# Expert batches of 416 places in place of 448 in a fused mLSTM, mixture-of-experts and MLP kernel

## The chip, the core and the metric

The kernel runs on one core of one Trainium2 chip. The metric is the device time of one execution in microseconds (us); three executions of the kernel before took 549.67, 539.68 and 545.39 us, so the median is 545.39 us.

## The reference

Three layers follow each other, all in float32. An mLSTM layer (2 batches, 8 heads, 768 steps, head size 40) gives 1536 tokens of 320 numbers. A mixture of 8 experts then routes each token to two of them, and a dense MLP of width 2048 with a gated ReLU6 closes:

```python
noisy_logits = x @ w_gate + log1p(exp(x @ w_noise)) * noise      # 1536 x 8
top2 = argpartition(-noisy_logits, 2, axis=1)[:, :2]
top2_w = softmax over the two chosen logits
for e in range(8):
    for k in range(2):
        mask = top2[:, k] == e
        h = maximum(x[mask] @ w1[e], 0)                          # 320 -> 1024
        out[mask] += top2_w[mask, k, None] * (h @ w2[e])         # 1024 -> 320
h = out @ w_in                                                   # 320 -> 2048
y = (h * clip(h + 3, 0, 6) / 6) @ w_out                          # 2048 -> 320
```

How many tokens an expert gets depends on the data; 3072 choices fall on 8 experts, 384 each on the mean.

## The kernel before, in words

**Attention and routing.** The loop over 12 chunks of 128 tokens (64 steps of both batches) computes the mLSTM. Each chunk's tokens are written to a DRAM table `Xd`, and `route` (line 428) computes the two experts of each token and a place in each of them. `scatter` (line 412) writes the token's number into the DRAM table `tab` at that place. `CAP` (line 31) is the number of places of one expert. A token whose place is `CAP` or more goes into an overflow part of the table. `overflow` (line 944) holds code under a run-time condition, which handles such tokens in tiles of 128, one after the other; it runs only if some expert has tokens beyond its places.

**Experts.** A `unit` (line 732) is a batch of one expert: a list of tiles (first place, number of places), and `nf` steps of 128 hidden columns. There are 10 such units up to `M0` (line 754): expert 0's first 192 places, expert 1's first 256, expert 1's rest (192 places), experts 2 to 7 with all 448 places (tiles of 128, 128, 128 and 64), and expert 0's rest (256 places in two tiles). `gather` (line 764) fetches a tile's tokens with an indirect DMA issued by GpSimd into `XG`; `xsplit` (line 777) turns each tile with three TensorE transposes (line 783) and splits the result in a high half `XH` and a low half `XL`.

`L1` (line 836) is the first layer of one step: eight matmuls (line 846) with 128x128 stationary weights, in which all of the unit's places move (N columns: 448, 256 or 192). ScalarE writes the high half of the ReLU to `hb` (line 849), VectorE the low half (lines 852, 855 and 857). `L2` (line 868) is the second layer: for each tile of 128 places three matmuls with 320 moving columns, in which the stationary operand is the tile's high half (line 882), again the high half (line 883) and its low half (line 884). A last tile of 64 places takes two: line 886, whose 128 stationary columns are 64 high and 64 low halves side by side, and line 887 with the 64 high halves. For this `L1` lays the last tile's low half right behind the high halves (`u.half`, line 740).

The steps run in a fixed program order (lines 1214 to 1225): `L1` of a step, then `L2` of the step two before it (`LAG`), and between them background work that the tables of lines 1146 to 1213 attach to a step: weights of the next expert (`w_split`: DMA into a ring of four `raw` buffers, ScalarE copy, VectorE subtraction, lines 594 and 595), the conversion of the MLP's weights (`conv`), gathers and transposes of the next unit. At a unit's last step `finish` (line 893) copies the sums out of PSUM and writes them to the DRAM table `Yd` (line 919).

**The MLP.** Six units of 512 tokens follow. `ygather` (line 790) fetches each token's two expert rows from `Yd`, `combine` (line 801) adds them with their weights, and the steps are as above with 512 or, in the first unit, 256 moving columns.

Of the kernel before, what the change touches and what calls it, by code (L numbers as in the profile page):

```python
# [18 lines left out]
OP = mybir.AluOpType  # L19
# [6 lines left out]
DM = H * D  # L26
# [1 line left out]
F = 1024  # L28
FF = 2048
V1 = D + 1  # L30
CAP = 448
CUT = (6, 8)
PRE = (192, 256)
RAWB = 4
# [14 lines left out]
WS = ((-1, 0), (0, 3), (0, 4), (0, 5, 'h'), (1, 0, 'l'), (1, 1), (1, 1), (1, 3), (1, 5), (1, 7), (2, 1))  # L49
TROWS = CAP + 11 * 128  # L50
OVB = 22
# [17 lines left out]
def mlstm_moe_mlp(ctx, tc, qk, kv, on, gf, gf6, wg, nz, w1, w2, w_in, w_out, cf, cb, cs, ci, out):  # L69
    nc = tc.nc  # L70
    V, A, G, T = nc.vector, nc.scalar, nc.gpsimd, nc.tensor
# [8 lines left out]
    def bank(i, dt=F32):  # L80
        return ps.tile([128, 512], dt, name=f"bank{i}")
# [142 lines left out]
    def step(k=1):  # L224
        for _ in range(k):
            for g_ in list(gens):
                if next(g_, "end") == "end":
                    gens.remove(g_)
# [139 lines left out]
    Xd = dram.tile([SLOTS, XW], F32, name="Xd")  # L368
    Yd = dram.tile([OV + CAP * E, DM], F32, name="Yd")
    tab = dram.tile([TROWS * E, 1], I32, name="tab")  # L370
# [54 lines left out]
    def small(shape, name, dt=F32):  # L425
        return const.tile(shape, dt, name=name, bufs=2)

    def route(m):
# [57 lines left out]
        if m == 2:  # L486
            t = small([128, 1], "t7")
            V.tensor_scalar(t, pc[:, 0:1], float(8 * LATE), float(8 * (CAP - LATE)), OP.is_gt, OP.mult)
            yield
# [13 lines left out]
        if 2 * m < 4:  # L503
            hi = small([128, 2, 1], "hi")
            V.tensor_scalar(hi, pe[:, :, 0:1], float(8 * LATE), float(8 * (CAP - LATE)), OP.is_ge, OP.mult)
            yield
# [26 lines left out]
        if m == NT // 2 - 1:  # L533
# [7 lines left out]
            yield  # L541
            V.tensor_scalar(cni[:, 0], cni[:, 0], float(CAP), 0.0, OP.subtract, OP.max)
            yield
# [15 lines left out]
            yield  # L559
            V.scalar_tensor_tensor(SLY, SLE, float(CAP), SLY, OP.mult, OP.add)  # L560
            yield
# [170 lines left out]
    def unit(e, tiles, nf=8):  # L732
        u = U()
        u.e, u.tiles, u.nf = e, tiles, nf
        u.N = sum(n for _, n in tiles)
        u.off, o = [], 0
        for _, n in tiles:
            u.off.append(o)
            o += n
        u.half = u.N - 64 if tiles[-1][1] == 64 else None  # L740
        u.bg = {}
        u.xo = 0
        u.st = e % 2
        u.l1 = [0, 1, 7]
        return u

    full = [(0, 128), (128, 128), (256, 128), (384, 64)]
    first, first2 = [(0, 128), (128, 64)], [(0, 128), (128, 128)]
    rest, rest2 = [(192, 128), (320, 128)], [(256, 128), (384, 64)]
    units = [unit(0, first), unit(1, first2), unit(1, rest2)]  # L750
    units[1].xo = 2
    units += [unit(e, full) for e in range(2, E)] + [unit(0, rest)]
    units[3].xo = 2
    M0 = len(units)
    units += [unit(8 + t, [((4 * t + i) * 128, 128) for i in range(4)]) for g in range(2) for t in range(3)]
    for i, u in enumerate(units):
        u.i = i
        u.g, u.xb = (i - M0) // 3, i % 2 if i < M0 else (i - M0) % 3
        n = len(u.tiles)
# [56 lines left out]
    def weights(u, f):  # L816
        g = f % 8
        if u.e < 8:
            W1 = W2 = sets[u.st]
            o = 5120  # L820
        else:
            W1, W2, o = win(u.g), wout(u.g), 0
        c = [W1[:, x + g * 128:x + g * 128 + 128] for x in (0, 1024, 2048, 3072, 4096)]
        return c, W2[:, o + g * DM:o + g * DM + DM], W2[:, o + 2560 + g * DM:o + 2560 + g * DM + DM]
# [5 lines left out]
    def split_hb():  # L830
        while unsplit:
            hb, r, N = unsplit.pop(0)
            A.copy(hb[:, 0:N], r)  # L833
            V.tensor_tensor(hb[:, N:2 * N], r, hb[:, 0:N], OP.subtract)  # L834

    def L1(u, f, t0, t1):
        (h0, h1, l0, l1, st), _, _ = weights(u, f)
        c0, N = u.off[t0], sum(n for _, n in u.tiles[t0:t1])
        p = bank(u.l1[nl1[0] % len(u.l1)])[:, 0:N]
        nl1[0] += 1  # L840
        xh, xl = [t[:, :, c0:c0 + N] for t in (XH[u.xb], XL[u.xb])]
        ops = [(h0, xh[:, 0]), (h0, xl[:, 0]), (l0, xh[:, 0]),
               (h1, xh[:, 1]), (h1, xl[:, 1]), (l1, xh[:, 1]),
               (st, xh[:, 2]), (st, xl[:, 2])]
        for i, (a, b) in enumerate(ops):
            T.matmul(p, a, b, start=(i == 0), stop=(i == 7))  # L846
        hb = wp.tile([128, 1024], F32R, name="hb", bufs=3)
        if u.e < 8:
            A.activation(hb[:, 0:N], p, AF.Relu)  # L849
            step()  # L850
            if u.half is None:
                V.scalar_tensor_tensor(hb[:, N:2 * N], p, 0.0, hb[:, 0:N], OP.max, OP.subtract)
            else:
                o = u.half
                V.scalar_tensor_tensor(hb[:, N:N + 64], p[:, o:N], 0.0, hb[:, o:N], OP.max, OP.subtract)  # L855
                step()
                V.scalar_tensor_tensor(hb[:, N + 64:2 * N], p[:, 0:o], 0.0, hb[:, 0:o], OP.max, OP.subtract)
        else:
            r = late.tile([128, 512], F32, name="r6", bufs=2)[:, 0:N]
            A.activation(r, p, AF.Relu, bias=three)  # L860
            V.scalar_tensor_tensor(r, r, 6.0, p, OP.min, OP.mult)  # L861

            split_hb()
            unsplit.append((hb, r, N))
        step()
        return hb

    def L2(u, f, t0, t1, hb, tiles=None):
        if any(h is hb for h, _, _ in unsplit):
            split_hb()  # L870
        _, wh, wl = weights(u, f)
        N = sum(n for _, n in u.tiles[t0:t1])
        if f == 0 and t0 == 0:
            u.acc = [bank(b) for b in (2, 3, 4, 6)[:len(u.tiles)]]
        s, t = f == 0, f == u.nf - 1
        for i in tiles or range(t0, t1):
            n, o = u.tiles[i][1], u.off[i] - u.off[t0]
            if n == 128:
                h = hb[:, o:o + 128]
                lo = N + o + (64 if u.half is not None else 0)  # L880
                p = u.acc[i][:, 0:DM]
                T.matmul(p, h, wh, start=s, stop=False)  # L882
                T.matmul(p, h, wl, start=False, stop=False)  # L883
                T.matmul(p, hb[:, lo:lo + 128], wh, start=False, stop=t)  # L884
            else:
                T.matmul(u.acc[i][:, 0:DM], hb[:, o:o + 128], wh, start=s, stop=False, skip_group_check=True)  # L886
                T.matmul(u.acc[i][0:64, 0:DM], hb[:, o:o + 64], wl, start=False, stop=t, skip_group_check=True)  # L887

    outr = out.rearrange("(b k t) d -> k b t d", b=B, k=NT)

# [2 lines left out]
    def finish(u, tiles=None):  # L893
        for i, (s, n) in enumerate(u.tiles):
            if tiles and i not in tiles:
                continue
            if u.e >= 8:
                if not parts:
                    parts.append(wp.tile([128, 5120], F32, name="SA1"))
                part = parts[0][:, s // 128 * DM:(s // 128 + 1) * DM]  # L900
            if u.e >= 8 and u.g == 0:

                if i % 2:
                    V.tensor_scalar(part, u.acc[i][:, 0:DM], 1.0 / 6.0, None, OP.mult)
                else:
                    A.mul(part, u.acc[i][:, 0:DM], 1.0 / 6.0)
                continue
            y = wp.tile([128, DM], F32, name="yo", bufs=4)
            if u.e < 8:
                if n == 64:  # L910
                    y2 = wp.tile([64, DM], F32, name="yo2", bufs=1)
                    A.copy(y2, u.acc[i][64:128, 0:DM])
                    V.tensor_tensor(y[0:64], u.acc[i][0:64, 0:DM], y2, OP.add)
                elif i % 2:
                    V.tensor_copy(y, u.acc[i][:, 0:DM])
                else:
                    A.copy(y, u.acc[i][:, 0:DM])
                r = OV + (7 - u.e) * CAP + s
                nc.sync.dma_start(Yd[r:r + n], y[0:n])
            else:  # L920
                V.scalar_tensor_tensor(y, u.acc[i][:, 0:DM], 1.0 / 6.0, part, OP.mult, OP.add)  # L921
                k = s // 128

                for b in range(B):
                    (A if b and u is units[-1] else nc.sync).dma_start(outr[k, b], y[rows[b]])
# [145 lines left out]
    n = NT - 2  # L1071
# [142 lines left out]
    for u in units:  # L1214
        if u.i == M0 - 2:
            overflow()
        for t, (f, lo, hi) in enumerate(u.steps):
# [6 lines left out]
            for fn, a in u.bg.get(t, []):  # L1224
                fn(*a)
    v, w = hbs
    L2(*v, (0, 1, 2))
    L2(*w, (0, 1))
    finish(units[-1], (0, 1))
    L2(*v, (3,))  # L1230
    L2(*w, (2, 3))
# [66 lines left out]
```

## Time and profile before

| | |
|---|---|
| three runs | 549.67, 539.68, 545.39 us; median 545.39 us |
| span of the profiled execution, first to last instruction | 546.7 us |
| TensorE (PE) matmuls | 512.1 us, 94% of the span, 4159 instructions |
| VectorE (DVE) | 346.8 us, 63% |
| ScalarE (ACT) | 227.2 us, 42% |
| GpSimd (POOL) | 133.6 us, 24% |
| attention and routing | 0 to 122.2 us |
| ten expert units | 122.2 to 362.1 us |
| six MLP units | 362.1 to 546.7 us |

No more is known of the profiled execution's time than its span. The page rests on one execution; PE's busy time overlaps from one matmul to the next, so that what a matmul costs is read from the distance of two starts, not from its duration. PEld is the load of the stationary operand, which runs beside the matmuls.

### The profile page before, as it was taken

The page shows a single profiled execution, that of the slowest core. Times are in us where ns is not written, and L with a number is a line of the kernel's source. Part 1 is how long each engine was busy: PE and PEld are TensorE (multiplying, and loading weights), DVE is VectorE, ACT ScalarE, POOL GpSimd, SP SyncE. Part 2 cuts the span into 40 slices and gives each one's busy share as a digit, 9 for nine tenths or more (in the row PEclk, how much of TensorE's full clock was granted, in tenths as well). Part 3 has the DMA queues.
Part 4 walks back from the last instruction along what each step waited for, and adds up shares of the span by engine and source line. Part 5 has one row for each costly group of instructions (what it writes and reads, how often), then busy time and mean ns, then how long its engine had stood idle before and what let it go on. Part 6 is the DMA issues. An engine that isn't in the chain of part 4 may idle for free. (4 is left out here: it accounts for less than half of the span.)

```text
span 546.7 us, 10810 instructions
## 1 busy us (share of the span) xinstructions
PE 512.1 (94%) x4159; PEld 455.3 (83%) x4159; DVE 346.8 (63%) x841; ACT 227.2 (42%) x469; POOL 133.6 (24%) x164
## 2 busy tenths in 40 slices
PE   4898989896959999999999999999999999999996
PEld 1476767675959999999999999989989989999985
DVE  5178786667645587878787878457698434343433
ACT  5123534233524354545454544246563333333321
POOL 5163464463530320202020002258600100000000
PEclk9798555568879999999999999999999999999999
DMA  8668788524186379787878768785931700011011
GB/s 237 165 185 232 182 154 148 114 93 117 41 269 214 111 272 285 281 289 274 285 276 290 253 174 295 237 271 172 320 110 74 217 0 1 1 25 24 13 37 49
DMA packets 47207, 92.75 MB, mean 170 GB/s; under 512 B 7488, under 2 KB 30880, under 8 KB 47152
## 3 DMA queue, kind: packets, MB, share of 16 engines
q1 hardware_dynamic: 39020, 68.97, 41.9%
q0 software_dynamic: 6464, 19.94, 12.0%
q10 hardware_dynamic: 1668, 3.12, 1.9%
q8 instruction: 33, 0.54, 0.4%
q14 instruction: 22, 0.18, 0.1%
HBM read 68.73 MB, written 23.07 MB: 168 GB/s over the span
## 5 line engine op out<-in xcount | busy, mean ns | idle before, releaser
L861 DVE SCALAR_TENSOR_TENSOR r<-r,bank 128x512 f32<-128x512 f32 (+1 forms) x56 | 34.2, 610 | 79.8 <-ACT r L860 79.4
L846 PE MATMUL bank<-XH,SB 128*128 128x448 f32 (+3 forms) x280 | 78.2, 350 | 0.3 <-PEq L946 0.3
L849 ACT ACTIVATE hb<-bank 128x448 fp32r<-128x448 f32 (+2 forms) x80 | 37.3, 468 | 93.1 <-PE bank L846 77.8
L860 ACT ACTIVATE r<-bank,cft 128x512 f32<-128x512 f32 (+1 forms) x56 | 35.1, 627 | 95.6 <-PE bank L846 90.0
L846 PE MATMUL bank<-XL,SB 128*128 128x448 f32 (+3 forms) x192 | 68.4, 356 | 0.0
L773 POOL DMA_INDIRECT XG<-Xd,idx x32 | 32.8, 1026 | 138.2 <-PE bank L783 108.4
L882 PE MATMUL bank<-SB,hb 128*128 128x320 f32 x192 | 62.4, 325 | 1.0 <-ACT hb L833 1.0
L882 PE MATMUL bank<-SA,hb 128*128 128x320 f32 x192 | 61.0, 317 | 0.0
L884 PE MATMUL bank<-SB,hb 128*128 128x320 f32 x192 | 60.0, 313 | 0.0
L883 PE MATMUL bank<-SB,hb 128*128 128x320 f32 x192 | 59.7, 311 | 0.0
L884 PE MATMUL bank<-SA,hb 128*128 128x320 f32 x192 | 59.6, 310 | 0.1
L883 PE MATMUL bank<-SA,hb 128*128 128x320 f32 x192 | 59.4, 309 | 0.0
L846 PEld LDWEIGHTS bank<-XH,SB 128*128 128x128 f32 x280 | 51.0, 191 | 5.1 <-issue 0.6
L846 PE MATMUL bank<-XH,SA 128*128 128x448 f32 (+2 forms) x200 | 52.4, 335 | 0.0
L846 PE MATMUL bank<-XL,SA 128*128 128x448 f32 (+2 forms) x120 | 40.1, 335 | 0.1
L846 PEld LDWEIGHTS bank<-XL,SB 128*128 128x128 f32 x192 | 36.6, 190 | 2.8
L882 PEld LDWEIGHTS bank<-SB,hb 128*128 128x128 f32 x192 | 36.6, 191 | 2.4 <-ACT hb L833 1.2
L846 PEld LDWEIGHTS bank<-XH,SA 128*128 128x128 f32 x200 | 36.0, 193 | 2.1 <-ACT XH L784 0.4
L855 DVE SCALAR_TENSOR_TENSOR hb<-bank,hb 128x64 fp32r<-128x64 f32 x64 | 14.1, 220 | 36.8 <-ACT hb L849 36.8
L882 PEld LDWEIGHTS bank<-SA,hb 128*128 128x128 f32 x192 | 36.3, 189 | 1.3
L883 PEld LDWEIGHTS bank<-SB,hb 128*128 128x128 f32 x192 | 36.6, 191 | 0.8
L883 PEld LDWEIGHTS bank<-SA,hb 128*128 128x128 f32 x192 | 36.3, 189 | 1.1
(198 smaller groups left out, 1148.4 us busy)
## 6 DMA issues: line engine op xcount, KB each, us to landing
raw<-in_w_dram SPq DMA_DIRECT2D x18, 640.0 KB
raw<-in_w_dram SPq DMA_DIRECT2D x18, 512.0 KB
qk<-in_qk_dram SPq DMA_DIRECT2D x22, 240.0 KB
craw<-in_w_in_dram SPq DMA_DIRECT2D x8, 640.0 KB
craw<-in_w_out_dram SPq DMA_DIRECT2D x8, 640.0 KB
raw<-in_w_dram SPq DMA_DIRECT2D x18, 256.0 KB
Yd<-yo SPq DMA_DIRECT2D x24, 160.0 KB
kv<-in_kv_dram SPq DMA_DIRECT2D x11, 324.0 KB
```

What stands on the lines that cost most here:

```text
L773: G.indirect_dma_start(out=XG[0:n, (u.xo + i) % 4, :], out_offset=None, in_=Xd[0:CUT[u.i] * 128] if early else Xd[:, :], in_offset=bass.In ...
L846: T.matmul(p, a, b, start=(i == 0), stop=(i == 7))
L849: A.activation(hb[:, 0:N], p, AF.Relu)
L855: V.scalar_tensor_tensor(hb[:, N:N + 64], p[:, o:N], 0.0, hb[:, o:N], OP.max, OP.subtract)
L860: A.activation(r, p, AF.Relu, bias=three)
L861: V.scalar_tensor_tensor(r, r, 6.0, p, OP.min, OP.mult)
L882: T.matmul(p, h, wh, start=s, stop=False)
L883: T.matmul(p, h, wl, start=False, stop=False)
L884: T.matmul(p, hb[:, lo:lo + 128], wh, start=False, stop=t)
```

## The change

Each expert has 416 places. The full units have tiles of 128, 128, 128 and 32 places; expert 1's rest has 128 and 32 (160 places), expert 0's rest 128 and 96 (224 places); the first parts of experts 0 and 1 stay at 192 and 256. A last tile of 32 places is handled as the last tile of 64 was: its high and low halves stand in 64 stationary columns (line 887 of the changed kernel), its high halves alone in 32 (line 888). A tile of 96 is handled as one of 128. The program's instructions stand in the same order and number on every engine; what differs is their sizes. Lines behind 740 are one further down.

```diff
-CAP = 448
+CAP = 416
...
-        u.half = u.N - 64 if tiles[-1][1] == 64 else None
+        u.tail = tiles[-1][1] if tiles[-1][1] < 96 else 0
+        u.half = u.N - u.tail if u.tail else None
...
-    full = [(0, 128), (128, 128), (256, 128), (384, 64)]
+    full = [(0, 128), (128, 128), (256, 128), (384, 32)]
     first, first2 = [(0, 128), (128, 64)], [(0, 128), (128, 128)]
-    rest, rest2 = [(192, 128), (320, 128)], [(256, 128), (384, 64)]
+    rest, rest2 = [(192, 128), (320, 96)], [(256, 128), (384, 32)]
...
-                V.scalar_tensor_tensor(hb[:, N:N + 64], p[:, o:N], 0.0, hb[:, o:N], OP.max, OP.subtract)
+                V.scalar_tensor_tensor(hb[:, N:N + u.tail], p[:, o:N], 0.0, hb[:, o:N], OP.max, OP.subtract)
                 step()
-                V.scalar_tensor_tensor(hb[:, N + 64:2 * N], p[:, 0:o], 0.0, hb[:, 0:o], OP.max, OP.subtract)
+                V.scalar_tensor_tensor(hb[:, N + u.tail:2 * N], p[:, 0:o], 0.0, hb[:, 0:o], OP.max, OP.subtract)
...
-            if n == 128:
-                h = hb[:, o:o + 128]
-                lo = N + o + (64 if u.half is not None else 0)
-                p = u.acc[i][:, 0:DM]
+            if n >= 96:
+                h = hb[:, o:o + n]
+                lo = N + o + u.tail
+                p = u.acc[i][0:n, 0:DM]
                 T.matmul(p, h, wh, start=s, stop=False)
                 T.matmul(p, h, wl, start=False, stop=False)
-                T.matmul(p, hb[:, lo:lo + 128], wh, start=False, stop=t)
+                T.matmul(p, hb[:, lo:lo + n], wh, start=False, stop=t)
             else:
-                T.matmul(u.acc[i][:, 0:DM], hb[:, o:o + 128], wh, start=s, stop=False, skip_group_check=True)
-                T.matmul(u.acc[i][0:64, 0:DM], hb[:, o:o + 64], wl, start=False, stop=t, skip_group_check=True)
+                T.matmul(u.acc[i][0:2 * n, 0:DM], hb[:, o:o + 2 * n], wh, start=s, stop=False, skip_group_check=True)
+                T.matmul(u.acc[i][0:n, 0:DM], hb[:, o:o + n], wl, start=False, stop=t, skip_group_check=True)
...
-                if n == 64:
+                if n < 96:
                     y2 = wp.tile([64, DM], F32, name="yo2", bufs=1)
-                    A.copy(y2, u.acc[i][64:128, 0:DM])
-                    V.tensor_tensor(y[0:64], u.acc[i][0:64, 0:DM], y2, OP.add)
+                    A.copy(y2[0:n], u.acc[i][n:2 * n, 0:DM])
+                    V.tensor_tensor(y[0:n], u.acc[i][0:n, 0:DM], y2[0:n], OP.add)
                 elif i % 2:
-                    V.tensor_copy(y, u.acc[i][:, 0:DM])
+                    V.tensor_copy(y[0:n], u.acc[i][0:n, 0:DM])
                 else:
-                    A.copy(y, u.acc[i][:, 0:DM])
+                    A.copy(y[0:n], u.acc[i][0:n, 0:DM])
```

## Rows read from the trace of the kernel before

**Rows 1.** Page, part 1: busy us, share of the span, instructions.

```profile
span 546.7 us, 10810 instructions
PE 512.1 (94%) x4159; PEld 455.3 (83%) x4159; DVE 346.8 (63%) x841; ACT 227.2 (42%) x469; POOL 133.6 (24%) x164
```

**Rows 2.** Busy time by stage: from:to, us, engines' busy us, PEclk, DMA share, GB/s.

```profile
0.00:122.20 122.20, 104.99 (x1655) 75.13 (x1655) 79.26 (x243) 43.33 (x133) 56.21 (x71) 0.69 0.69 169
122.20:142.80 20.60, 15.29 (x111) 14.33 (x111) 13.54 (x79) 8.17 (x19) 10.86 (x17) 0.83 0.37 104
142.80:166.40 23.60, 17.96 (x118) 17.23 (x117) 12.06 (x28) 8.87 (x17) 7.72 (x10) 0.86 0.57 176
166.40:181.10 14.70, 14.70 (x120) 14.47 (x119) 8.61 (x27) 6.59 (x15) 2.73 (x3) 1.00 0.65 211
...
234.20:261.60 27.40, 27.40 (x166) 25.84 (x166) 21.71 (x44) 13.55 (x22) 3.91 (x4) 1.00 0.82 281
...
345.10:362.10 17.00, 17.00 (x132) 16.98 (x130) 7.70 (x19) 6.30 (x16) 8.23 (x9) 1.00 0.69 227
```

**Rows 3.** Waits from 181 to 362 us: who for whom, us, times, longest.

```profile
ACT hb L849 <- PE bank L846: 62.0, 40, 3.2
POOL raw L697 <- DMA Wi<-clr: 33.6, 1, 33.6
...
POOL yg L794 <- PE bank L846: 12.3, 1, 12.3
...
PE bank L846 <- PEq L946: 0.3, 1, 0.3
```

**Rows 4.** Chain that ended last, pieces of line 846: start us, us.

```profile
338.46 1.61 PE bank L846 x8
...
342.02 1.65 PE bank L846 x8
...
352.48 0.96 PE bank L846 x8
...
466.01 1.84 PE bank L846 x8
```

**Rows 5.** PE in order of time, expert 1's rest: start us, us, instruction.

```profile
179.52 0.25 PE L846 MATMUL bank<-XH,SB 128*128 128x192 f32 x1
179.61 0.27 PE L846 MATMUL bank<-XL,SB 128*128 128x192 f32 x1
...
180.39 0.33 PE L882 MATMUL bank<-SB,hb 128*128 128x320 f32 x1
```

**Rows 6.** PE in order of time, expert 7: end of a second layer.

```profile
337.72 0.31 PE L883 MATMUL bank<-SB,hb 128*128 128x320 f32 x1
337.87 0.31 PE L884 MATMUL bank<-SB,hb 128*128 128x320 f32 x1
338.01 0.30 PE L886 MATMUL bank<-SB,hb 128*128 128x320 f32 x1
338.15 0.31 PE L887 MATMUL bank<-SB,hb 128*64 128x320 f32 x1
338.30 0.36 PE L846 MATMUL bank<-XH,SB 128*128 128x448 f32 x1
```

**Rows 7.** PE in order of time, expert 5: transposes of 128 and of 64 rows.

```profile
279.91 0.37 PE L846 MATMUL bank<-XL,SB 128*128 128x448 f32 x1
280.12 0.49 PE L783 MATMUL bank<-cft,XG 128*128 128x128 f32 x3
280.36 0.39 PE L882 MATMUL bank<-SB,hb 128*128 128x320 f32 x1
...
283.46 0.37 PE L846 MATMUL bank<-XL,SB 128*128 128x448 f32 x1
283.75 0.40 PE L783 MATMUL bank<-cft,XG 64*128 64x64 f32 x3
284.08 0.42 PE L882 MATMUL bank<-SB,hb 128*128 128x320 f32 x1
```

**Rows 8.** POOL in order of time, first fetch of expert results.

```profile
351.97 1.02 POOL L794 DMA_INDIRECT yg<-Yd,SLY  x1 [12.34 <-PE bank L846]
```

**Rows 9.** DMA issues: median us to landing last.

```profile
raw<-Wi POOLq DMA_DIRECT2D x4, 512.0 KB, 5.1
...
XG<-Xd,idx POOLq DMA_INDIRECT x32, 4.6
```

## Prediction

> **What bounds the kernel now.** I read the shares of the span first [rows 1]: the reader is to see that TensorE (PE) is busy for 94% and no other engine for more than 63%. That is a mean over unlike stages, so the busy times by stage come next [rows 2]. Attention and the first two expert units (0 to 166.4 us) have gaps on PE and a granted clock of 0.69 to 0.86, so these stretches are partly at the lower of the two clock levels (1.2 GHz) and partly at 2.4 GHz. From 166.4 us on the granted clock is 1.00, and in the expert units PE is busy for the whole of each stretch: 14.70 of 14.70 us, 27.40 of 27.40, 17.00 of 17.00. Beside it VectorE works 21.71 of 27.40 us and ScalarE 13.55; the DMA engines are busy for 0.82 of the time. The waits of 181 to 362 us [rows 3] say the same from the other side: PE has one entry, 0.3 us, while ScalarE waits 62.0 us for PE's first layer. No entry in that view has PE waiting for `hb`, for split weights or for gathered tokens. So in the stretch in which the change acts, PE's own instruction stream is the time, and a microsecond less of it should be a microsecond less of the span. The chain that ended last agrees: in that stretch it holds groups of eight first-layer matmuls, which I use as the price list [rows 4].
>
> **The change, part by part.** The order and number of instructions stay on every engine, SP's and POOL's DMA queues among them; nothing is moved past another and no wait is added. Only sizes change, so the question is which sizes PE pays for.
>
> *First layer of experts 2 to 7.* One step is eight matmuls of N moving columns. Eight take 1.84 us at 512 columns, 1.61 at 448 (1.65 beside transposes) and 0.96 at 256 [rows 4]. From 512 to 448 that is 0.23 us for 64 columns, from 448 to 256 it is 0.65 for 192: 3.6 and 3.4 ns per column of a step, close to a straight line. 32 columns fewer are then 0.108 to 0.115 us a step, and I take 0.11. Six units of eight steps: 48 x 0.11 = 5.3 us. 416 lies between two measured sizes, so I give this term only 5.1 to 5.5.
>
> *First layer of expert 1's rest, 192 to 160 columns.* The straight line would give 192 columns 0.96 - 64 x 0.0034 = 0.74 us; measured are 180.39 - 179.52 = 0.87 [rows 5]. So at this width something that doesn't shrink with the columns already sets the pace, about 0.109 us a matmul; the load of eight different stationary operands of 128 columns is the candidate, and these keep their size. I take 0. If the line went on below, it would be 8 x 0.11 = 0.9 us; a loss I exclude, as the loads are unchanged.
>
> *First layer of expert 0's rest, 256 to 224 columns.* The line gives 0.85 us, the floor just seen 0.87, so a step falls from 0.96 to 0.87: 8 x 0.09 = 0.7 us. But behind this unit the MLP starts, and the fetch of its rows begins only at 351.97 [rows 8], 6.9 us into the unit, released by results of expert 7, so it doesn't move with this unit's steps. If the fetch has no slack, the 0.7 us turns into a wait of PE at 362; I take 0.5, with 0 and 0.9 as ends.
>
> *Second layer.* Matmuls start 0.145 us apart with 320 moving columns whether 128 or 64 stationary columns are used: lines 883, 884 and 886 with 128, line 887 with 64 start at 337.72, 337.87, 338.01, 338.15, and the next one at 338.30 [rows 6]. Line 886 goes from 128 to 64 stationary columns and line 887 from 64 to 32; both still move 320. The tile of 96 keeps three matmuls of 320. I take 0 for all 56 steps with a short last tile (six units and expert 1's rest) and the 8 with the tile of 96. No row shows a 32-column load between 128-column ones with these operands. The ends are below: a loss if the array has to empty, a gain if narrower loads were cheaper. They are rivals.
>
> Here a page speaks against the change. In the trace a narrower column group costs nothing: from line 887, with 64 columns, back to 128 are 0.15 us, as within a run of 128 [rows 6]. The Trainium skill, TensorEngine Tiling (Array Packing), section Key Properties, says that changing the tiling mode drains TensorE. By that rule line 887 should have cost something before, and rows 6 disagree; where rows of the array and not columns are cut, rows 7 do show a cost. So the sum by the rows has no term here; by the rule it would have one, which is the first rival.
>
> *Transposes.* Three transposes of a 128-row tile lie between two starts 0.45 us apart (279.91 to 280.36), of a 64-row tile 0.62 (283.46 to 284.08) [rows 7]: the short tile is 0.17 us dearer, though it moves half the columns. Seven short tiles go from 64 to 32 rows, one tile from 128 to 96. Half the columns again could save some hundredths each; 96 rows could cost the 0.17 that 64 rows do. Ends -0.5 and +0.5 us, value 0.
>
> *Everything else is beside PE.* ReLU copies and low halves get shorter, gathers fetch 32 rows fewer, `Yd` gets 32 rows fewer per unit: all on engines with idle time in every unit [rows 2], so nothing on the path. The cover is PE's stream: a unit of 27.4 us becomes 26.5, and the same weight traffic in it lifts the DMA share from 0.82 to 0.85, VectorE's share to about 0.8. If that cover were gone, units would stay at 27.4 (second rival).
>
> *Sum.* 5.3 + 0 + 0.5 + 0 + 0 = 5.8 us. The profiled span is 546.7 us, and no more of that execution's time is known; 546.7 - 5.8 = 540.9. The span lies 1.3 us above the median of the three runs shown, so the same 5.8 us from 545.39 gives 539.6 us, 1.1% less.
>
> **The rivals.**
>
> *The array empties at the narrow tile: slower.* Place: lines 887 and 888 of the changed kernel. Before, a step goes from 128 to 64 stationary columns and back; now from 128 to 64, to 32 and back, one change more. Price: the 64-row transposes show 0.17 us for a change there and back, 0.085 each [rows 7]; the other end is a full wait for the matmul before, its duration of 0.31 less the usual distance of 0.145, or 0.165 [rows 6]. With 56 steps that is 4.8 to 9.2 us, and net -1.0 to +3.4 us: 544.4 to 548.8 in terms of the median. It decides from 5.8 / 56 = 0.104 us per step; above that the change is a loss. For it speaks that no row has the new sizes; against it that line 887 shows nothing of the kind. By the drain that the Trainium skill names (TensorEngine Tiling (Array Packing), Key Properties), this is the case that would come.
>
> *The gain is hidden: weights or VectorE set the unit's length.* Then experts 2 to 7 stay at their length and only the 0.5 us remain: 544.9 us. For it speaks the DMA share of 0.82, the highest of any stage [rows 2]. Against it: PE has no wait for weights there [rows 3], and every unit has 5.7 us of VectorE time left.
>
> *The overflow code runs: much slower.* It decides at the 417th place of any expert. I worked out the reference's routing from its inputs: the experts get 376, 381, 395, 394, 356, 387, 373 and 410 tokens, and the first parts of experts 0 and 1 leave 6 and 7 places empty. The largest is 410 of 416, so nothing overflows unless the data are others. The price would be a tile of 128 in eight steps, each of which waits for weights that nothing has fetched before: 8 x 5.1 us for a landing and 4.6 for the gather [rows 9], at least 45 us, some 585 us or more in all.
>
> *Narrower loads are cheaper.* If a second-layer matmul's distance went with its stationary columns, the pair of lines 887 and 888 would fall by half, 0.145 us, in 56 steps: 8.1 us more, 531.5 us. Rows 6 speak against it: 64 columns take as long as 128.
>
> **How the numbers follow.** Forecast 0.72, the emptying array 0.13, the hidden gain 0.09, overflow 0.03, cheaper loads 0.03. The predicted time is the forecast's, 539.6 us. The forecast's own terms are sure to about 1 us; what makes the range wide is that three runs of one kernel lie between 539.68 and 549.67, so a median of the changed kernel can fall some 6 us on either side. The first two rivals lie within that or just above it. I give 533.0 to 547.0. A change of 2%, 10.9 us, is about what a measurement of this kernel can tell from none, and 5.8 us is half of it: within 2% 0.88, faster by more 0.07 (cheaper loads 0.03, and 0.04 of a forecast measured on a lucky pair), slower by more 0.05 (overflow 0.03, and 0.02 of the emptying array).
>
> **What would show it.** Right: eight first-layer matmuls of 416 columns take 1.50 us; units of experts 3 to 5 last 26.5 us in place of 27.4; eight of 160 columns still take 0.87 and eight of 224 about 0.87; lines 887 and 888 start 0.145 us apart and the next first layer 0.15 behind; PE still has no wait of weight between 181 and 362 us; the stretch before 166 us is unchanged but for the run's own scatter. Wrong: a distance of 0.2 us or more around line 888 (the array empties); waits of PE for `hb` or of ScalarE for raw weights in the units (gain hidden); a new wait before the first MLP step that is over 0.5 us longer (the fetch had no slack); instructions of lines 985 to 1016 that ran (overflow).

## The result and the profile after

Over 20 runs each, the changed kernel has a median of 538.84 us (533.87 to 546.32) and the kernel before 546.05 us (538.57 to 553.33), 7.2 us apart. The ratio, which counts only the executions within 1.5% of the fastest of their kernel, is 0.9891 with a 95% interval of 0.9856 to 0.9925: 1.1% less, 5.9 us (4.1 to 7.9), against a forecast of 5.8 us and 539.6 us. The gain lies inside the 2% bound.

The profiled execution of the changed kernel took 544.72 us. The page's first part answers to [rows 1]:

```profile
span 542.9 us, 10810 instructions
PE 500.5 (92%) x4159; PEld 448.1 (83%) x4159; DVE 343.8 (63%) x841; ACT 225.2 (41%) x469; POOL 137.4 (25%) x164
```

PE has 11.6 us less, more than the change can take away. In attention and routing alone, which the change leaves as they were, the same 1655 matmuls were busy for 96.83 us in place of 104.99, at a granted clock of 0.79 in place of 0.69. So the stages must be looked at apart. The busy times by stage answer to [rows 2]; the bounds are the first matmuls of the expert units:

```profile
0.00:121.69 121.69, 96.83 (x1655) 68.15 (x1655) 78.58 (x244) 43.66 (x133) 57.20 (x72) 0.79 0.68 170
121.69:142.79 21.10, 16.18 (x110) 15.15 (x111) 12.63 (x71) 8.04 (x19) 11.28 (x19) 0.82 0.48 93
142.79:168.13 25.34, 20.33 (x116) 19.48 (x117) 13.26 (x35) 8.96 (x18) 7.09 (x6) 0.76 0.53 167
168.13:182.78 14.65, 14.65 (x121) 14.24 (x119) 8.34 (x28) 6.35 (x15) 2.79 (x3) 1.00 0.68 214
...
233.77:260.13 26.36, 26.36 (x166) 25.46 (x165) 21.35 (x44) 13.25 (x22) 4.22 (x4) 1.00 0.86 289
...
340.46:356.88 16.42, 16.42 (x131) 16.34 (x130) 7.39 (x19) 6.09 (x16) 7.11 (x8) 1.00 0.69 219
356.88:389.87 32.99, 30.83 (x232) 29.76 (x231) 23.86 (x65) 18.29 (x45) 25.68 (x27) 1.00 0.87 276
```

Three rows of the same view of the kernel before, between the exact starts of the units, belong beside the last three: expert 4, expert 0's rest, the first MLP unit:

```profile
234.17:261.59 27.42, 27.42 (x166) 25.86 (x165) 21.73 (x44) 13.55 (x22) 3.91 (x4) 1.00 0.82 281
...
345.13:362.09 16.96, 16.96 (x131) 16.94 (x130) 7.66 (x19) 6.29 (x16) 8.23 (x9) 1.00 0.69 227
362.09:393.69 31.60, 30.55 (x232) 29.73 (x231) 23.80 (x66) 19.04 (x47) 21.20 (x25) 1.00 0.82 256
```

The reader is to see four things. A full expert's unit has gone from 27.42 to 26.36 us with PE busy throughout; expert 1's rest stayed at 14.65 (14.70 before); expert 0's rest went from 16.96 to 16.42. The DMA share in a full unit rose from 0.82 to 0.86, as the same weights come in less time. The stretch before 168 us is 1.7 us longer than before, at other granted clocks, though its units kept their sizes. And the first MLP unit is 1.4 us longer, which nothing in the forecast accounts for.

The prices come next. PE in order of time in expert 4 and the start of expert 5, the end of a second layer and a first layer with 416 columns, answers to [rows 6]:

```profile
259.69 0.31 PE L885 MATMUL bank<-SA,hb 128*128 128x320 f32 x1
259.84 0.31 PE L887 MATMUL bank<-SA,hb 128*64 128x320 f32 x1
259.99 0.31 PE L888 MATMUL bank<-SA,hb 128*32 128x320 f32 x1
260.13 0.35 PE L847 MATMUL bank<-XH,SB 128*128 128x416 f32 x1
...
261.44 0.35 PE L847 MATMUL bank<-XL,SB 128*128 128x416 f32 x1
261.63 0.30 PE L883 MATMUL bank<-SA,hb 128*128 128x320 f32 x1
```

Lines 887 and 888, with 64 and 32 stationary columns, start 0.15 us apart, and the next first layer 0.14 behind: no emptying, no saving. Eight first-layer matmuls take 261.63 - 260.13 = 1.50 us. The same can be read in the chain of waits, which answers to [rows 4] (416 columns, then the 224 of expert 0's rest, start and length in us):

```profile
334.12 1.50 PE bank L847 x8
...
340.63 0.88 PE bank L847 x8
```

Three transposes of the 32-row tile, between the last first-layer matmul ahead of them and the second layer behind, in the same view as [rows 7]:

```profile
254.73 0.35 PE L847 MATMUL bank<-XL,SA 128*128 128x416 f32 x1
255.01 0.37 PE L784 MATMUL bank<-cft,XG 32*128 32x32 f32 x3
255.31 0.41 PE L883 MATMUL bank<-SA,hb 128*128 128x320 f32 x1
```

From start to start of the matmuls around them they take 0.58 us, against 0.62 with 64 rows in the kernel before. In the changed kernel a tile of 128 rows takes 0.43 (251.28 to 251.71) and the one of 96 rows 0.38 (335.27 to 335.65). So tiles of 64 and 32 rows are the dearer ones, one of 96 is not, and from 64 to 32 little changes.

### The profile page after: what moved, and what is told of

Its sections match the earlier page's. It is cut to its first block, busy times and chain, and to the rows that moved or that the text cites. A ratio compares the mean times of both kernels' runs of the same rounds, so it can differ in the third digit from the quotient of the medians.

```text
span 542.9 us, 10810 instructions
## 1 busy us (share of the span) xinstructions
PE 500.5 (92%) x4159; PEld 448.1 (83%) x4159; DVE 343.8 (63%) x841; ACT 225.2 (41%) x469; POOL 137.4 (25%) x164
## 5 line engine op out<-in xcount | busy, mean ns | idle before, releaser
L847 PE MATMUL bank<-XH,SB 128*128 128x416 f32 (+3 forms) x280 | 77.8, 348 | 4.9 <-issue 4.6
L850 ACT ACTIVATE hb<-bank 128x416 fp32r<-128x416 f32 (+4 forms) x80 | 35.6, 447 | 95.4 <-PE bank L847 76.5
L847 PE MATMUL bank<-XL,SB 128*128 128x416 f32 (+3 forms) x192 | 68.3, 356 | 0.0
L774 POOL DMA_INDIRECT XG<-Xd,idx x32 | 33.9, 1059 | 134.6 <-PE bank L784 112.3
L847 PEld LDWEIGHTS bank<-XH,SB 128*128 128x128 f32 x280 | 52.1, 196 | 10.0 <-issue 6.0
L847 PE MATMUL bank<-XH,SA 128*128 128x416 f32 (+2 forms) x200 | 51.7, 331 | 1.0 <-ACT XH L785 1.0
L847 PE MATMUL bank<-XL,SA 128*128 128x416 f32 (+2 forms) x120 | 39.7, 331 | 0.0
L883 PEld LDWEIGHTS bank<-SB,hb 128*128 128x128 f32 x192 | 36.5, 190 | 3.5 <-ACT hb L834 2.6
L884 PEld LDWEIGHTS bank<-SB,hb 128*128 128x128 f32 x192 | 36.5, 190 | 0.6
L885 PEld LDWEIGHTS bank<-SB,hb 128*128 128x128 f32 x192 | 36.3, 189 | 0.5 <-DVE hb L835 0.4
```

The source lines that it names most:

```text
L774: G.indirect_dma_start(out=XG[0:n, (u.xo + i) % 4, :], out_offset=None, in_=Xd[0:CUT[u.i] * 128] if early else Xd[:, :], in_offset=bass.In ...
L885: T.matmul(p, hb[:, lo:lo + n], wh, start=False, stop=t)
```

## Experiments

### The first layer alone

Everything of the kernel before, but seven of eight first-layer matmuls of experts 2 to 7 with 416 columns:

```diff
-            T.matmul(p, a, b, start=(i == 0), stop=(i == 7))
+            n = 416 if i and N == 448 else N
+            T.matmul(p[:, 0:n], a, b[:, 0:n], start=(i == 0), stop=(i == 7), skip_group_check=True)
```

> The kernel before, with one edit: in experts 2 to 7, seven of the eight first-layer matmuls of a step move 416 of the 448 columns (the first one moves all 448). Tiles, transposes, second layer, gathers and stores keep their old sizes, as do both parts of experts 0 and 1. The last 32 places of these experts get only the first of the eight products. Theory A (PE pays for moving columns and for nothing else of the change): a step's eight matmuls take 1.61 - 7 x 0.0138 = 1.51 us, the units of experts 3 to 5 last 27.42 - 0.78 = 26.64 us, and the kernel gains 48 x 0.097 = 4.7 us, ratio to the kernel before 0.991. Rival B (a good part of the gain came from the shorter transposes, the narrow second layer or the smaller DMAs): the units keep more than 27.0 us and the ratio is over 0.995.

Measured: ratio 0.9894, interval 0.979 to 0.9998 (6 runs), on its own too wide to tell 0.991 from 0.995. The trace is sharper. PE in order of time, one step of expert 3:

```profile
229.66 0.36 PE L847 MATMUL bank<-XH,SB 128*128 128x448 f32 x1
229.86 0.35 PE L847 MATMUL bank<-XL,SB 128*128 128x416 f32 x1
...
231.18 0.31 PE L883 MATMUL bank<-SB,hb 128*128 128x320 f32 x1
...
232.79 0.36 PE L847 MATMUL bank<-XH,SA 128*128 128x448 f32 x1
```

Eight first-layer matmuls take 1.52 us, and the units of experts 3 to 5 begin at 206.19, 232.79, 259.39 and end at 285.99: 26.60 us each, 0.82 less than before. Eight sevenths of that is 0.94 of the 1.06 us that the whole change gives a unit. So the moving columns of the first layer are nearly all of it, and theory A holds.

### Wide loads for the narrow tile

The changed kernel with the old stationary widths in the short tile's second layer:

```diff
-                T.matmul(u.acc[i][0:2 * n, 0:DM], hb[:, o:o + 2 * n], wh, start=s, stop=False, skip_group_check=True)
-                T.matmul(u.acc[i][0:n, 0:DM], hb[:, o:o + n], wl, start=False, stop=t, skip_group_check=True)
+                T.matmul(u.acc[i][:, 0:DM], hb[:, o:o + 128], wh, start=s, stop=False, skip_group_check=True)
+                T.matmul(u.acc[i][0:64, 0:DM], hb[:, o:o + 64], wl, start=False, stop=t, skip_group_check=True)
```

> The changed kernel, with the two second-layer matmuls of the tile of 32 places loading 128 and 64 stationary columns as they did before, in place of 64 and 32 (the further columns hold other halves, whose sums go to rows that nobody reads or add a product of low halves). The 320 moving columns stay. Theory A (narrow loads cost and save nothing): starts stay 0.145 us apart, units of experts 3 to 5 stay at 26.36 us, ratio to the kernel before 0.989, as the changed kernel. Rival (the array empties when the column mode changes): units get shorter by 8 x 0.085 = 0.7 us or more. Rival (narrow loads are cheaper): units get longer, by up to 8 x 0.145 = 1.2 us.

Measured: ratio to the kernel before 0.9894 (0.9843 to 0.9944), as the changed kernel. PE in order of time in expert 4's unit:

```profile
229.15 0.31 PE L885 MATMUL bank<-SB,hb 128*128 128x320 f32 x1
229.29 0.31 PE L887 MATMUL bank<-SB,hb 128*128 128x320 f32 x1
229.44 0.32 PE L888 MATMUL bank<-SB,hb 128*64 128x320 f32 x1
229.59 0.35 PE L847 MATMUL bank<-XH,SA 128*128 128x416 f32 x1
```

The distances are 0.14 to 0.15 us as with the narrow loads, and the units of experts 3 and 4 last 26.41 and 26.42 us (starts at 200.06, 226.47 and 252.89) against 26.36. Both rivals on the narrow tile fall: with these wide loads the emptying array asked for units 0.7 us shorter or more, the cheaper load for units up to 1.2 us longer, and 0.05 us is there.

### Two probes of the floor in expert 1's rest

The prediction took the load of 128 stationary columns as what holds 160 moving columns at the pace of 192. One kernel makes the load narrow, the other the moving operand narrower still, each in seven of eight first-layer matmuls of that unit:

```diff
+            m = 64 if i and u.i == 2 else 128
+            T.matmul(p[0:m], a[:, 0:m], b, start=(i == 0), stop=(i == 7), skip_group_check=True)
```

> The changed kernel, with seven of the eight first-layer matmuls of expert 1's rest (160 moving columns) loading only 64 of the 128 stationary columns; half of that unit's hidden numbers get only the first of the eight products. Theory A (below some 230 columns the load of 128 stationary columns sets the distance of 0.11 us): the distance falls towards what the moving columns ask for, 160 x 0.43 ns + 13 ns = 0.08 us, so that a step's eight take about 0.67 us in place of 0.87. Rival B (the floor is one of issue or of the matmul itself): it stays at 0.87.

```diff
+            n = 96 if i and u.i == 2 else N
+            T.matmul(p[:, 0:n], a, b[:, 0:n], start=(i == 0), stop=(i == 7), skip_group_check=True)
```

> The changed kernel, with seven of the eight first-layer matmuls of expert 1's rest moving 96 of its 160 columns; the other 64 places of that unit get only the first of the eight products. Loads keep their 128 stationary columns. Theory A (the load sets the distance there): a step's eight still take 0.85 to 0.88 us and the unit stays at 14.65 us. Rival B (moving columns still pay with an offset): seven matmuls lose 64 x 0.43 ns each, 0.19 us a step, so that eight take about 0.68 us and the unit 13.1 us.

PE in order of time, a step with narrow loads:

```profile
168.63 0.23 PE L848 MATMUL bank<-XH,SB 128*128 128x160 f32 x1
168.71 0.24 PE L848 MATMUL bank<-XL,SB 128*64 128x160 f32 x1
...
169.22 0.49 PE L784 MATMUL bank<-cft,XG 128*128 128x128 f32 x3
```

and a step with 96 moving columns and full loads:

```profile
164.36 0.24 PE L848 MATMUL bank<-XH,SB 128*128 128x160 f32 x1
164.43 0.25 PE L848 MATMUL bank<-XL,SB 128*128 128x96 f32 x1
...
165.19 0.53 PE L784 MATMUL bank<-cft,XG 128*128 128x128 f32 x3
```

With 64 stationary columns eight take 169.22 - 168.63 = 0.59 us, with 96 moving columns 165.19 - 164.36 = 0.83, where the changed kernel takes 0.86 (173.28 to 174.14 in its profile). In seven of the eight, taking away 40% of the moving columns gave 0.03 us, halving the loads 0.27. The whole unit says it more sharply: 12.49 us with narrow loads (162.64 to 175.13) and 14.62 with narrow moving operands (155.34 to 169.96), against 14.65; what the second probe gains in the first layer it loses right behind, in the second. Theory A holds in both, a little stronger than expected in the first (0.67 expected). The one run of each, 535.55 and 530.61 us, says nothing about this at the scatter of the kernel's times.

The narrow matmuls also write 64 output rows in place of 128, and the probe doesn't part this from the load. The loads' own records (PEld) do shorten, from 0.19 to 0.13 us, first in the changed kernel, then in the probe:

```profile
173.29 0.19 PEld L847 LDWEIGHTS bank<-XL,SB 128*128 128x128 f32 x1
```

```profile
168.64 0.13 PEld L848 LDWEIGHTS bank<-XL,SB 128*64 128x64 f32 x1
```

The Trainium skill, TensorE: Matmul & The Clock Gate, section LDWEIGHTS (loading the stationary operand), gives a load's time in ns as about its columns divided by 1.2, an estimate of 107 ns for 128; the measured pace of about 0.11 us a matmul agrees with that.

### How much slack the first fetch of the MLP has

The changed kernel with two of eight first-layer matmuls left out in expert 0's rest, the unit that covers the fetch:

```diff
+        if u.i == M0 - 1:
+            ops = ops[0:2] + ops[3:5] + ops[6:8]
```

> The changed kernel, with two of the eight first-layer matmuls left out in expert 0's rest (the two with the low halves of the weights), so that this unit has 8 x 0.22 = 1.8 us less PE work. Theory A (the first fetch of the MLP has no slack behind that unit): the unit shrinks from 16.4 to about 14.7 us, but PE's waits between its end and the MLP's regular steps grow by 1.5 to 1.8 us, and the time stays that of the changed kernel, ratio to the kernel before 0.989. Rival B (the fetch has slack): these waits stay near the 1.4 us of the changed kernel's profile and the whole 1.8 us is gained, ratio 0.986.

Measured: ratio 0.9884 (0.9803 to 0.9964), which doesn't separate 0.989 from 0.986. In the trace the unit runs from 332.35 to 348.75: 16.40 us, as long as with all its matmuls. PE in order of time near its end:

```profile
343.59 0.27 PE L849 MATMUL bank<-XL,SA 128*128 128x224 f32 x1
344.85 0.55 PE L784 MATMUL bank<-cft,x 128*128 128x128 f32 x3 [0.98 <-DVE x L807]
...
347.51 0.52 PE L784 MATMUL bank<-cft,x 128*128 128x128 f32 x3 [0.37 <-DVE x L807]
...
348.75 0.28 PE L849 MATMUL bank<-XH,raw 128*128 128x256 f32 x1
```

The 1.8 us came back as waits of the MLP's first transposes for the rows that line 807 combines from the fetched results: inside the unit, where those transposes stand, not behind it as I had written. Theory A holds for the time: nothing was gained, because the fetch is the bound. It begins at 339.88 us, as POOL's instructions in order of time show, and the MLP's first matmul follows 8.87 us later:

```profile
339.88 1.03 POOL L795 DMA_INDIRECT yg<-Yd,SLY  x1 [12.30 <-PE bank L849]
```

### The changed kernel a second time

> The changed kernel once more, unchanged, for a second profile. Theory A (the 33.0 us of the MLP's first unit in the first profile, against 31.6 us before, came from a single wait that one execution happened to have): the unit lasts 31.3 to 31.7 us here. Rival B (the change itself lengthens that unit): it lasts 32.5 us or more again. Expert units as in the first profile, 26.36 us for experts 3 to 5.

One run, 538.37 us, beside one run of the kernel before of 538.64 us; where one kernel's times lie 12 us and more apart, such a pair doesn't show the change. Busy time by stage (expert 1's rest, expert 4, expert 0's rest, the first MLP unit):

```profile
162.73:177.38 14.65, 14.65 (x120) 14.24 (x119) 8.33 (x28) 6.35 (x15) 2.77 (x3) 1.00 0.69 208
228.38:254.74 26.36, 26.36 (x167) 25.46 (x165) 21.34 (x44) 13.26 (x22) 4.23 (x4) 1.00 0.87 289
335.07:352.07 17.00, 16.74 (x131) 16.31 (x130) 7.36 (x19) 6.18 (x16) 7.12 (x8) 1.00 0.66 208
352.07:383.50 31.43, 30.36 (x232) 29.73 (x231) 24.38 (x66) 18.94 (x47) 22.94 (x26) 1.00 0.89 282
```

The first MLP unit lasts 31.43 us, and 31.41 or 31.42 in the profiles of the five experiments above, so the 33.0 of the first profile belonged to one execution. In that first profile ScalarE sat idle for 2.48 us ahead of copying a first layer's sums out of PSUM, as its instructions in order of time show:

```profile
374.00 0.47 ACT L861 ACTIVATE r<-bank,cft 128x256 f32<-128x256 f32 x1 [2.48 <-PE bank L784]
```

What held it is not settled: the view names PE, but a first layer had ended well before 374.00. On the other hand, expert 0's rest lasts 17.00 us here, with a wait for the fetch like the one of the experiment above:

```profile
350.85 0.52 PE L784 MATMUL bank<-cft,x 128*128 128x128 f32 x3 [0.26 <-DVE x L807]
```

What differs between the two executions is when the fetch begins. POOL in order of time, the first profile and then this one:

```profile
348.00 1.03 POOL L795 DMA_INDIRECT yg<-Yd,SLY  x1 [12.32 <-DMA Yd<-yo]
```

```profile
343.29 1.03 POOL L795 DMA_INDIRECT yg<-Yd,SLY  x1 [13.01 <-PE bank L847]
```

The profiles up to here give, in us:

| kernel | columns of expert 0's rest | fetch begins, from the unit's start | unit | from the fetch's start to the MLP's |
|---|---|---|---|---|
| before | 256 | 6.84 | 16.96 | 10.12 |
| first layer alone | 256 | 7.66 | 16.97 | 9.31 |
| changed | 224 | 7.54 | 16.42 | 8.88 |
| changed, second time | 224 | 8.22 | 17.00 | 8.78 |
| wide loads | 224 | 7.86 | 16.66 | 8.80 |
| narrow loads in expert 1's rest | 224 | 7.45 | 16.42 | 8.97 |
| narrow moving operands there | 224 | 7.91 | 16.70 | 8.79 |
| short rest | 224, six matmuls | 7.53 | 16.40 | 8.87 |

PE alone needs 16.42 us for 224 columns and 16.96 for 256, and the MLP never starts sooner than 8.8 us behind the fetch's start: the later of the two ends the unit. The fetch waits for expert 7's results to be stored, whose last copy out of PSUM ends 3.8 us into the unit, before and after; from there to the fetch it was 3.0 us before, and 3.8 and 4.4 in the two profiles of the changed kernel. As it began late with the old tiles too (7.66), these runs don't show that the change delays it.

### The overflow's price

The changed kernel with 384 places, three tiles of 128 per expert:

```diff
-CAP = 416
+CAP = 384
...
-    full = [(0, 128), (128, 128), (256, 128), (384, 32)]
+    full = [(0, 128), (128, 128), (256, 128)]
...
-    rest, rest2 = [(192, 128), (320, 96)], [(256, 128), (384, 32)]
+    rest, rest2 = [(192, 128), (320, 64)], [(256, 128)]
```

> The changed kernel with 384 places per expert: three tiles of 128 for experts 2 to 7, 128 places for expert 1's rest, 192 for expert 0's rest. By the reference's routing five experts then have more tokens than places (388, 395, 394, 387 and 410 of 384), so the code for the overflow runs for five tiles of 128. Theory A (the rival of the prediction, with its price): the units of experts 3 to 5 fall by 8 x 0.12 us for 32 columns and 8 x 0.29 us for the two matmuls of the short tile, to about 23 us, but each overflow tile costs at least 45 us, so the kernel ends above 720 us. Rival B (an overflow tile costs under 10 us): it would be near 550 us or below.

One run, 740.4 us. Busy time by stage, expert 4, and from expert 6's start to expert 7's, between which the overflow code runs:

```profile
216.50:239.61 23.11, 22.97 (x148) 22.61 (x146) 19.63 (x33) 12.16 (x20) 3.83 (x3) 1.00 0.97 322
262.68:511.16 248.48, 149.54 (x482) 105.32 (x481) 27.87 (x62) 27.79 (x70) 4.74 (x5) 0.55 0.33 98
```

A full unit is 3.3 us shorter than with 416 places, as expected. The long stretch less one such unit is 248.5 - 23.1 = 225.4 us for five tiles, 45 us each, at a granted clock of 0.55, that is mostly at 1.2 GHz. The condition on the 417th place was no empty one: the next step down loses 200 us. PE in order of time at the start of the second overflow tile and at two of its steps:

```profile
345.04 0.87 PE L996 MATMUL bank<-cft,yg 128*128 128x128 f32 x3 [12.09 <-DMA yg<-Xd,oix]
...
352.65 1.41 PE L1013 MATMUL bank<-yg 128*128 128x320 f32 x2 [0.70 <-DMA yg<-in_w_dram]
...
356.37 1.41 PE L1013 MATMUL bank<-yg 128*128 128x320 f32 x2 [0.74 <-DMA yg<-in_w_dram]
```

A step takes about 3.8 us (3.72 here), of which PE waits 0.6 to 0.9 for its weights (from the second step on), and ahead of each tile PE waits some 12 us for the gathered rows.

## Why the prediction was right, point by point

**The bound.** That PE's stream is the time in the expert units was shown by the result and by the first experiment: what was taken from it there shortened a full unit by as much, with no new wait of PE (one entry of 0.3 us between 182.78 and 340.46 us, as before), though the DMA share rose to 0.86.

**First layer of experts 2 to 7.** Forecast 0.11 us a step, 0.88 a unit. A full unit lost 1.06. Summed from start to start over expert 4's unit, the first layer went from 13.10 to 12.10 us, the transposes from 1.06 to 1.04 and the second layer from 13.26 to 13.22. So nearly all of it is the first layer, and the term was a little small: it took 1.61 us as the price of every step before, which only half of the steps had. The others had cost 1.64 to 1.70 (1.65 in [rows 4]), and all but one now take 1.49 to 1.51; why those steps were dearer was not tried. From the first matmul of expert 2 to that of expert 0's rest, the six units are 6.3 us shorter (163.99 to 157.68), in place of 5.3.

**Expert 1's rest.** Forecast 0, measured 0.05 us. The two probes show that the floor goes with the stationary columns and not with the moving ones; that it is their load, and not the output rows, is the nearest reading and wasn't tested apart.

**Expert 0's rest.** Forecast 0.87 for eight matmuls with 224 columns, from 0.96; measured 0.88, and a unit of 16.42 us in one profile. But the slack of the fetch was the doubtful part, and rightly: the second profile has 17.00 us, no gain at all. In the five profiles that have this unit as the changed kernel has it, the gain on 16.96 is 0.54 twice, 0.30, 0.26 and -0.04, 0.3 on the mean; 0 to 0.5 would have been the better statement. The reading that the fetch begins 6.9 us into the unit held for one execution: in those five it began at 7.45 to 8.22.

**Second layer and transposes.** Forecast 0, with ends on both sides; the distances of 0.14 to 0.15 us and the wide-load experiment bear it out. The drain that the Trainium skill names (TensorEngine Tiling (Array Packing), Key Properties) doesn't show in this case when only stationary columns change, at 64 or at 32. It may be what makes transposes of 32 and 64 rows 0.15 to 0.17 us dearer than those of 128 in the same kernel; no run here tells that. The fear that the tile of 96 rows costs what 64 rows do was wrong: it is cheaper than 128 rows (0.38 against 0.43).

**The sum.** From the first matmul of expert 1's rest to the end, the kernel before takes 546.7 - 166.4 = 380.3 us, the changed one 542.9 - 168.1 = 374.8 and, the second time, 536.6 - 162.7 = 373.9: 5.5 and 6.4 us less. The 5.8 us stand between them, but that is partly luck: a first-layer term 1.0 us too small was set off, in the first profile by 1.4 us of the long MLP unit, in the second by the 0.5 us that expert 0's rest did not gain. From the first matmul of expert 2 to the end the kernel before takes 365.6 us and the same five profiles 358.6 to 360.1, 5.4 to 7.0 less. And the measured 5.9, with its interval of 4.1 to 7.9, doesn't tell 5.8 from any of these.

**The range.** In the two profiles of the changed kernel, the scatter that made the range wide lies almost wholly ahead of the change: it reaches expert 1's rest at 168.1 us in one execution and at 162.7 in another, while what follows differs by 0.9 us.

**The rivals.** The emptying array and the cheaper load fell with the wide-load experiment. The hidden gain fell with the units' 26.36 us, but in small it is true of one unit: expert 0's rest is where the bound passes from PE to the fetch. The overflow didn't run. Its price of at least 45 us a tile was measured as 45, but not by the chain that was forecast: in place of eight landings of 5.1 us and a gather of 4.6, there are eight steps of 3.8 us (30 in all) and 13 to 15 around PE's wait for the gathered rows. That the two sums agree is luck.

## What to carry to other kernels

Price a matmul by the distance of two starts, at three sizes or more, and look for the size at which the line ends: here moving columns pay at 0.43 ns each down to about 230 (an estimate from 0.120 us a matmul at 256 and 0.110 at 224), below which the load of 128 stationary columns sets 0.11 us, so that cutting a 192-column batch gives nothing. A unit that covers someone else's transfer pays back what it loses as soon as the cover is used up, so its term belongs in the sum as "nothing up to". And when runs scatter by more than the change is worth, compare stretches of traces from the first changed instruction on.

## What the runs showed that I had not expected

Halving the loaded columns took eight matmuls with 160 moving columns from 0.86 to 0.59 us, 0.073 us each and close to the 0.069 us that 160 columns make at 0.43 ns; the 13 ns that I added on top of the columns, from wider matmuls, are hardly there. A transposed tile of 32 rows costs more than one of 128 (0.58 against 0.43 us from start to start), and one of 96 rows less (0.38). And the code for an overflow tile ran mostly at the lower clock level (0.55 granted), so the clock may be a part of its 45 us; how large a part was not tried.
